# First expert unit by eight products, attention output with block pairs on the partitions, later weight loads

## The chip, the cores and the metric

The kernel runs on one core of one Trainium2 chip. The metric is the device time of one execution in microseconds (us). Before the change the median of three runs is 710.21 us (707.49 to 710.64). One execution more was recorded by the hardware profiler; all rows of a profile below come from that one.

## What is computed

Attention over 8 batches, 8 heads, 576 positions and 64 features a head, followed by a layer of 8 experts in which each token uses one expert.

```python
scores = q @ k.T / sqrt(64)           # heads 0-3: the last 32 positions
attn   = softmax(where(mask, scores, -1e9))   # heads 4-7: every 4th of the last 128
x      = (attn @ v) -> (B, S, 512)    # heads side by side

logits = x @ w_gate                   # 8 experts
local  = sigmoid(x @ w_local)
for s in order:                       # per batch
    e = argmax(logits[s]) if s == 0 or local[s] < 0.5 else e_of_the_token_before
    out[s] = softmax(logits[s])[e] * (relu(x[s] @ w1[e]) @ w2[e])
```

w1 of an expert is 512 x 1024, w2 is 1024 x 512, both float32 (2 MB each). A token's expert depends on its predecessor's where `local` is 0.5 or more, so that the routing is a scan along the sequence.

## The kernel before, in words

**Attention.** The program runs over 32 pairs of heads (`NPB`; four pairs a batch, two of plain heads and two of dilated heads, the latter sorted by position modulo 4 so that their windows are contiguous too). A pair has 9 query blocks of 64 positions (`NB`); a block sees 96 keys: 32 before it and its own 64. The loop at lines 1016 to 1044 runs 34 iterations n. In each:

- `scores(n)` (L284): for each block and head of the pair a product of keys and queries with the mask added, then the exponential on ScalarE. The blocks go in two groups (`UNITS`, 0 to 4 and 5 to 8).
- `values(n-1)` (L339): for each block and head the product of the probabilities (96 keys x 64 queries) with the values (96 x 65; the 65th column is ones and gives the sum). The two heads of the pair lie on partitions 0-63 and 64-127 of the PSUM tile `pv`. VectorE takes the reciprocals (L355) and multiplies (L356) into the tile `x`.
- `turn` (L360), in every second iteration from n = 3: transposes of `x` of two pairs (half a batch: 4 heads, 256 features), nine of 128 x 128, with ScalarE's copies into `xt`, the features of two batches. After four turns (two batches, a group g of four) the routing of the group is put into a queue (`route`, L976).
- `store` (L376): `x` of two pairs goes to the DRAM tensors `xd`, whose rows are tokens with 256 features (1024 bytes). With heads on the partitions each row is written in two pieces of 512 bytes.
- `load(n+3)` on SP's queue: keys and queries of a pair (592 KB) and values (292.5 KB). A block also needs the last 32 values of the block before it: GpSimd copies these "shared rows" within the tile (L247), as the last step of the load, so the copy of pair n+3 stands on GpSimd's queue in iteration n.

**Routing.** The queue `waiting` holds the steps of a group's routing (logits, L384, then the scan, the counting and the placing of tokens), each with an estimated cost. `gap(SHARE)` puts steps between the parts of an iteration as far as a credit allows; after the attention `work_gap()` puts one step, or a group that goes together, between two products of the experts. A second queue, `soon`, holds VectorE's sums, which `work_gap` takes when the queue of steps is empty or has an odd length.

**Experts.** Tokens are collected by expert into units. Units of kind "pair" are 256 tokens. They are computed with seven products in place of eight (`chain`, L820): the two operands are cut into quarters, sums of quarters are formed on VectorE (`sums_of_weights` for w1 and w2, `sums_right` in `features` for the tokens, called xc, `sums_left` for the hidden values, called hc; L766 to L775), and results are added up on VectorE (L891, L965). `hidden(u)` is relu(x w1), `output(u)` the product with w2; `features(u)` transposes the gathered rows of x (`xg`, by indirect DMAs on GpSimd, L797) into `xe`. Units 0 and 1 (`FIRST` = 2) take tokens of the first four batches only, so they can be formed while the attention still runs: after the second routing `early_tokens` puts their eight gathers into `rows`, of which each iteration of the attention issues one. The other units wait for the whole routing (`late_tokens`). A unit of kind "full" has 128 tokens and is computed directly, "half" has 64.

**Weights.** Three slots hold w1 (`raw1`) and w2 (`raw2`). The first w1 of slot 0 comes in four parts of 512 KB (`load_first`, n = 4, 6, 8, 10). At n = `NPB - 4` = 28 SP issues w2 of unit 0 and w1 of unit 1, 2 MB each; from n = 28 on, one sum of w1 of unit 0 is put into each iteration; at n = 30 come the features of unit 0, ahead of that iteration's end; w2 of unit 1 follows the attention.

**What sets the order.** TensorE, VectorE and GpSimd execute in the order of the program text; SP's queue issues DMAs in the order of the text as well. So every call above has a fixed place in the queue of each engine that it uses.

After the attention: `run_hidden(0)` with the sums of w2 of unit 0, features(1), `run_output(0)` with the sums of w1 of unit 1, `run_hidden(1)`, `output(1)`, in whose fourth product `feed` loads the weights of the next units and issues features(2); then the loop over the other units.

Of the kernel before, what the change touches and what calls it, by code (L numbers as in the profile page):

```python
# [38 lines left out]
UNITS = ((0, 5), (5, 9))  # L39
CB = 3  # L40
# [152 lines left out]
def whole(ctx, tc, exact, bad, qk, v, wgl, w1, w2, con, msk, qmk, out, cst, wg, ones):  # L193
# [35 lines left out]
    rec = once.tile([P, NPB, NB], F32, name="rec")  # L229
# [14 lines left out]
    def load_values(n):  # L244
        vt = vts[n % AHEAD]
        nc.sync.dma_start(out=vt[WIN:].rearrange("p u i e -> p (u i e)"), in_=v[n])
        nc.gpsimd.tensor_copy(vt[:WIN, :, 1:], vt[QB:, :, :NB - 1])  # L247
# [91 lines left out]
    def values(n):  # L339

        vt = loaded[n][2]
        if n % 2 == 0:
            xs[n // 2] = xp.tile([P, NB, 2, DH], F32, name="x")
        x = xs[n // 2]
        pr = prob.pop(n)
        for a, z in UNITS:
            pv = bank([P, z - a, VW], "pv")
            for i in range(a, z):
                c, p = next((c, p) for c, p in reversed(pr) if c <= i)
                for u in range(2):  # L350
                    nc.tensor.matmul(pv[u * QB:(u + 1) * QB, i - a], lhsT=p[:, u, (i - c) * QB:(i - c + 1) * QB],  # L351
                                     rhs=vt[:, u, i], start=True, stop=True, tile_position=(0, u * QB),
                                     skip_group_check=True)
            r = rec[:, n, a:z]
            nc.vector.reciprocal(r, pv[:, :, DH])  # L355
            nc.vector.tensor_tensor(x[:, a:z, n % 2], pv[:, :, :DH],  # L356
                                    r.unsqueeze(2).to_broadcast([P, z - a, DH]), op=Alu.mult)
        del loaded[n]

    def turn(m):  # L360

        x = xs[m]
        b, g = divmod(m, 2)
        if m % (2 * GB) == 0:
            routes[b // GB] = dict(xt=xtp.tile([P, 2, GS, CH], F32, name="xt"))
        xt = routes[b // GB]["xt"]
        w = NB // 3
        for c in range(3):
            tp = bank([P, w, 2, QB], "tp")
            for i in range(w):  # L370
                nc.tensor.transpose(tp[:, i].rearrange("p u q -> p (u q)"),
                                    x[:, c * w + i].rearrange("p g d -> p (g d)"), ident)
            s = b % GB * S + c * w * QB
            nc.scalar.copy(xt[:, g, s:s + w * QB].rearrange("p (i q) u -> p i u q", i=w), tp)

    def store(m):  # L376
# [3 lines left out]
        to = xd[g][b * S:(b + 1) * S].rearrange("(i q) (u f) -> u q i f", q=QB, u=2)  # L380
        for u in range(2):
            nc.sync.dma_start(out=to[u], in_=x[u * QB:(u + 1) * QB].rearrange("q i g d -> q i (g d)"))

    def logits(g):  # L384
# [4 lines left out]
        for kk in range(DK):  # L389
            for c in range(NC):  # L390
                if kk < CH:
                    rhs = xt[:, 0, c * NQ:(c + 1) * NQ, kk]
                else:
                    b, s = divmod(c * NQ, S)
                    rhs = xt[:, 1, b * S:(b + 1) * S, kk - CH].rearrange("p (c j) -> p j c", c=DIL)
# [301 lines left out]
    units = [dict(kind="pair", col=2 * i, slot=i, late=False) for i in range(FIRST)]  # L697
# [47 lines left out]
    def work_gap(sums=True):  # L745
        if waiting:
            gap()
            sums = sums and len(waiting) % 2
        for _ in range(len(soon) > 4 and 2 or len(soon) > 0 if sums else 0):
            soon.pop(0)()  # L750
# [35 lines left out]

    def gather(u):
        now(rows_of(u))

    def rows_of(u):  # L790
# [10 lines left out]
        return [lambda j=j, g=g, what=what: part(j, g, what) for j in range(2 if units[u]["kind"] == "pair" else 1)  # L801
                for g, what in enumerate(("tok", "pos"))]

    def features(u):
# [3 lines left out]
        for j in range(2 if kind == "pair" else 1):  # L808
# [37 lines left out]
    def hidden(u):  # L846
# [3 lines left out]
        if kind == "half":  # L850
# [7 lines left out]
            nc.scalar.activation(h[:, 0:2].rearrange("p m t -> p (m t)"), t, Act.Relu)  # L858
            return
# [53 lines left out]
    def output(u):  # L913
        i, kind = units[u]["slot"], units[u]["kind"]
        h, w = ht.pop(u), raw2[i]
        if kind == "half":
# [17 lines left out]
            return  # L934
        if kind == "full":
# [40 lines left out]
    def route(g, slow):  # L976
        steps = [(logits, 0, True), (fresh, 3.0, True), (carry, 1.0, True), (carry_over, 0.5, True), (carry_in, 0.5, True),
                 (choose, 1.5, True), (gate, 1.5, False), (place, 0.5, True), (lanes_of, 1.3, False)]
        if slow:
            waiting.insert(0, (lambda: logits(g), 0, True))  # L980
# [35 lines left out]
    for n in range(NPB + 2):  # L1016
        if n < NPB:
            (scores_exact if exact else scores)(n)
        gap(SHARE)
        if 1 <= n <= NPB:  # L1020
            values(n - 1)
        if n == NPB - 4:
            soon.extend(sums_of_weights(0, False))
        if soon:
            soon.pop(0)()
# [9 lines left out]
        if n in (4, 6, 8, 10):  # L1035
            load_first(0, n // 2 - 2)
        if n == NPB - 4:
            weights(0, True)
            weights(1, False)
        if rows:  # L1040
            rows.pop(0)()
        if n == NPB - 2:
            assert len(rows) <= 4
            now(features(0))
# [14 lines left out]
    def check():  # L1059

        flat = rec.rearrange("p n i -> p (n i)")
        fine = stage.tile([P, D], F32, name="y", bufs=3)[:, :NPB * NB]
# [8 lines left out]
        nc.vector.tensor_scalar(all_fine, lp, float(P * NPB * NB), None, Alu.is_lt)  # L1071
# [7 lines left out]
    def run_hidden(u, push):  # L1079
        soon.extend(push)  # L1080
        for fits in hidden(u):
            work_gap(fits)
        flush()
# [29 lines left out]
    run_hidden(0, sums_of_weights(0, True))  # L1113
    first, then = units[0]["sums"][:2], units[0]["sums"][2:]
    now(first)
    then += features(1)
    now(then)
    run_output(0, sums_of_weights(1, False))
    run_hidden(1, sums_of_weights(1, True))
    now(units[1]["sums"])  # L1120
    for k, fits in enumerate(output(1)):
        work_gap(fits)
# [4 lines left out]
    weights(after[1], True)  # L1127
    third = next(u for u in range(NU) if units[u]["slot"] == 2)
    for u in range(FIRST, NU):
# [8 lines left out]
        else:  # L1138
            now(push)
# [26 lines left out]
def _chunks(w):  # L1166

    return w.reshape(2, 2, CH, DH, -1).transpose(0, 2, 1, 3, 4).reshape(DK, P, -1)
# [33 lines left out]
```

## Time and profile before

| what | before |
|---|---|
| median of three runs | 710.21 us (707.49 to 710.64) |
| the profiled execution | 706.11 us, span of its instructions 703.9 us |
| mean granted clock of TensorE | 0.979 |
| busy: TensorE (PE) / weight loads (PEld) | 671.1 us (95%) / 579.1 us (82%) |
| busy: VectorE (DVE) / ScalarE (ACT) / GpSimd (POOL) | 386.2 (55%) / 194.8 (28%) / 183.5 us (26%) |
| DMA | 126.59 MB, mean 180 GB/s |
| attention, with its last logits | up to 173.59 us |

How to read the rows. A line of a timeline gives the start, the length, the engine, the line of the kernel, the operation, the tiles as written<-read, the shapes and how many instructions were merged into it; in brackets stands how long the engine had been idle before it, and what ended that. A float32 product leaves two records (x36 for 18 products); a transpose leaves one. The lengths of TensorE's instructions overlap, so the cost of a run of them is the distance of its start to the start of what follows. A line of stretches gives the stretch, its length, the busy time of each engine with its number of instructions, the granted clock (1.00 is full speed), the share of the DMA engines and GB/s. In the page's slices each digit is a fortieth of the span, in tenths.

### The profile page before, as it was taken

The numbers are of one execution on the slowest core, as the hardware profiler recorded it, in microseconds if no ns is written. First come the engines' busy times: TensorE is split into PE (matmuls) and PEld (weight loads), VectorE is DVE, ScalarE is ACT, GpSimd is POOL, SyncE is SP. The second block draws the span as 40 slices with busy tenths as digits, with TensorE's granted clock in tenths as the row PEclk, the third lists the DMA queues.
The fourth block names the chain that finished last, engine by engine and source line by source line (L and its number), as shares of the span: only waits on it lengthen the run. The fifth ranks groups of instructions, "written<-read, shape, count | busy, mean of one in ns | idle before, by whom it ended". The sixth has DMA issues, their size and how long they took to land. (4 is left out here: it accounts for less than half of the span.)

```text
span 703.9 us, 14739 instructions
## 1 busy us (share of the span) xinstructions
PE 671.1 (95%) x6182; PEld 579.1 (82%) x6182; DVE 386.2 (55%) x768; ACT 194.8 (28%) x353; POOL 183.5 (26%) x162
## 2 busy tenths in 40 slices
PE   8999999979997979999999999999999999999994
PEld 6977788756986978999689999599998699996883
DVE  3547478566697558544274572547461828442632
ACT  3544344322311232312122322222222132121220
POOL 3222212230012430402371331513133323032101
PEclk9999999966999999999999999999999999999998
DMA  8999878893102677567262614754004556342201
GB/s 330 321 342 284 250 235 256 257 349 83 73 16 104 226 265 274 184 250 266 84 267 73 229 38 151 245 203 168 31 23 128 217 181 251 135 170 57 122 23 35
DMA packets 38475, 126.59 MB, mean 180 GB/s; under 512 B 4253, under 2 KB 22813, under 8 KB 34432
## 3 DMA queue, kind: packets, MB, share of 16 engines
q1 hardware_dynamic: 31552, 106.15, 43.7%
q0 software_dynamic: 6848, 19.41, 8.0%
q8 instruction: 51, 0.84, 0.5%
q14 instruction: 24, 0.20, 0.1%
HBM read 142.32 MB, written 19.40 MB: 230 GB/s over the span
## 5 line engine op out<-in xcount | busy, mean ns | idle before, releaser
L909 POOL DMA_INDIRECT out_dram<-y,tok x36 | 53.9, 1497 | 323.0 <-DVE y L965 177.5
L881 PE MATMUL hp<-xc,sum 128*128 128x128 f32 x768 | 91.5, 275 | 1.2 <-DVE sum L766 1.2
L950 PE MATMUL yp<-sum,hc 128*128 128x256 f32 x384 | 88.5, 380 | 3.8 <-DVE hc L766 3.4
L881 PEld LDWEIGHTS hp<-xc,sum 128*128 128x128 f32 x768 | 88.5, 192 | 1.4 <-DVE sum L766 1.4
L891 DVE TENSOR_TENSOR h<-hp,h 128x512 f32<-128x512 f32 x48 | 32.9, 689 | 100.1 <-PE hp L881 97.8
L950 PEld LDWEIGHTS yp<-sum,hc 128*128 128x128 f32 x384 | 72.6, 190 | 14.5 <-DVE hc L766 3.4
L881 PE MATMUL hp<-xe,raw 128*128 128x128 f32 x512 | 62.9, 276 | 2.5 <-ACT xe L813 2.5
L881 PEld LDWEIGHTS hp<-xe,raw 128*128 128x128 f32 x512 | 60.2, 192 | 5.2 <-ACT xe L813 2.8
L247 POOL COPY vt<-vt 32x1040 f32<-32x1040 f32 x32 | 34.3, 1073 | 108.0 <-DMA vt<-in_v_dram 86.1
L950 PE MATMUL yp<-raw,h 128*128 128x256 f32 x256 | 60.7, 380 | 0.0
L301 PEld LDWEIGHTS two<-kq 64*96 64x96 f32 x1152 | 53.5, 167 | 7.8 <-issue 7.1
L301 PE MATMUL two<-kq 64*96 64x64 f32 x1152 | 58.0, 254 | 0.0
L965 DVE SCALAR_TENSOR_TENSOR y<-yp,gate,y 128x256 f32<-128x256 f32 x48 | 23.1, 482 | 58.6 <-issue 33.3
L950 PEld LDWEIGHTS yp<-raw,h 128*128 128x128 f32 x256 | 47.3, 190 | 6.1 <-issue 0.4
L797 POOL DMA_INDIRECT xg<-xd,tok x40 | 45.5, 1137 | 23.4 <-PE yp L950 10.6
L306 DVE SCALAR_TENSOR_TENSOR pr<-two,mk 96x512 f32<-96x512 f32 x32 | 21.9, 685 | 52.7 <-ACT pr L308 39.6
L892 ACT ACTIVATE h<-h 128x512 f32<-128x512 f32 x48 | 30.2, 630 | 71.3 <-DVE h L891 64.0
L885 ACT COPY h<-hp 128x512 f32<-128x512 f32 x48 | 28.1, 586 | 74.5 <-PE hp L881 73.3
L797 POOL DMA_INDIRECT xg<-xd,pos x40 | 42.9, 1072 | 12.2 <-issue 11.0
L351 PE MATMUL pv<-vt,pr 96*64 96x65 f32 x1152 | 43.1, 231 | 0.0
L958 ACT ACTIVATE y<-yp,gate 128x256 f32<-128x256 f32 x48 | 22.8, 474 | 66.2 <-PE yp L950 65.1
L351 PEld LDWEIGHTS pv<-vt,pr 96*64 96x64 f32 x1152 | 38.5, 144 | 2.5 <-issue 0.7
(208 smaller groups left out, 1005.1 us busy)
## 6 DMA issues: line engine op xcount, KB each, us to landing
raw<-in_w_dram SPq DMA_DIRECT2D x48, 2048.0 KB
kq<-in_qk_dram SPq DMA_DIRECT2D x32, 592.0 KB
vt<-in_v_dram SPq DMA_DIRECT2D x32, 292.5 KB
xd<-x SPq DMA_DIRECT2D x32, 288.0 KB
raw<-in_w_dram SPq DMA_DIRECT2D x4, 512.0 KB
xg<-xd,tok POOLq DMA_INDIRECT x40
xg<-xd,pos POOLq DMA_INDIRECT x40
out_dram<-y,tok POOLq DMA_INDIRECT x36
```

The lines of the kernel that those rows point to most:

```text
L247: nc.gpsimd.tensor_copy(vt[:WIN, :, 1:], vt[QB:, :, :NB - 1])
L301: nc.tensor.matmul(sc[:KW, u, (i - a) * QB:(i - a + 1) * QB], lhsT=kt[h, i * QB:i * QB + KW], rhs=qt[h, i * QB:(i + 1) * QB], start=bool(a ...
L351: nc.tensor.matmul(pv[u * QB:(u + 1) * QB, i - a], lhsT=p[:, u, (i - c) * QB:(i - c + 1) * QB], rhs=vt[:, u, i], start=True, stop=True, ti ...
L797: nc.gpsimd.indirect_dma_start(out=x[:rows, g], out_offset=None, in_=xd[g] if units[u]["late"] else xd[g][:EARLY * GS], in_offset=bass.Ind ...
L881: nc.tensor.matmul(to[:, m], lhsT=a[:, m, kk], rhs=b[:, kk], start=first and m == 0 and kk == 0, stop=(kk == DK // 2 - 1), skip_group_chec ...
L885: nc.scalar.copy(at((0, 1, 3)[k]), of)
L891: nc.vector.tensor_tensor(at(k), of, at(k), op=Alu.add)
L892: nc.scalar.activation(at(k), at(k), Act.Relu)
L909: nc.gpsimd.indirect_dma_start(out=out, out_offset=bass.IndirectOffsetOnAxis(ap=of_unit(u, "tok", j), axis=0), in_=y, in_offset=None, boun ...
L950: nc.tensor.matmul(to, lhsT=a[:, m], rhs=b[:, m], start=first and m == 0, stop=(m == FK // 2 - 1), skip_group_check=True)
L958: nc.scalar.activation(at(k), of, Act.Copy, scale=of_unit(u, "gate", k // 2))
L965: nc.vector.scalar_tensor_tensor(at(k), of, of_unit(u, "gate", k // 2), at(k), Alu.mult, Alu.add)
```

## The change

- **x and values.** `x` becomes [128, 5 slots, 2 pairs, 2 heads, 64]: on partitions 0-63 lies block 2k, on 64-127 block 2k+1. The fifth slot has only block 8; its second half computes block 8 again. The groups are `HALVES`, slots 0-1 and 2-4.
- **turn** makes eight transposes of 128 x 128 and two of 64 x 128, and three copies without a permutation; `xt` has the tokens innermost. **store** issues one DMA for 512 tokens and one for 64, in rows of 1024 bytes. Logits read `xt` with a step of one element in place of two (for the dilated heads: four classes 144 elements apart in place of 288). The weights' features are ordered to match, on the host.
- **Shared rows**: `share(n)` is called after `scores(n)`, no longer in the load of pair n.
- **Unit 0** is of the new kind "plain": 256 tokens with all products, 32 of 256 columns for hidden (two accumulations a PSUM bank) and 16 of 512 for output, without sums; ScalarE scales the output.
- **Later**: the four parts of the first w1 at n = 11, 14, 17, 20; w1 of unit 1, then w2 of unit 0, at n = 33; features(0) at n = 33, before the turn; no sums in the attention.
- **Order of the first units**: features(1) after hidden(0), its sums in output(0); the first two hc sums of unit 1 before the rest of `soon`; of output(1) the last two products go behind hidden(2), features(3) and gather(4), and the load of w2 of unit 3 behind them.
- `work_gap` always takes a step of the routing, and a sum where that step's cost is below 1.2; the last group's logits are issued at once.

```diff
@@ values
-            xs[n // 2] = xp.tile([P, NB, 2, DH], F32, name="x")
+            xs[n // 2] = xp.tile([P, SLOTS, 2, 2, DH], F32, name="x")
...
-        for a, z in UNITS:
-            pv = bank([P, z - a, VW], "pv")
-            for i in range(a, z):
-                c, p = next((c, p) for c, p in reversed(pr) if c <= i)
+        for a, z in HALVES:
+            pv = bank([P, z - a, 2, VW], "pv")
+            for k in range(a, z):
                 for u in range(2):
...
+                    for h in range(2):
+                        i = min(2 * k + h, NB - 1)
+                        c, p = next((c, p) for c, p in reversed(pr) if c <= i)
+                        nc.tensor.matmul(pv[h * QB:(h + 1) * QB, k - a, u], lhsT=p[:, u, (i - c) * QB:(i - c + 1) * QB],
+                                         rhs=vt[:, u, i], start=True, stop=True, tile_position=(0, h * QB),
+                                         skip_group_check=True)
@@ turn
+        s = b % GB * S
+        full = S // P * P
+        for c in range(CH):
+            tp = bank([P, S // P, P], "tp")
+            for k in range(S // P):
+                nc.tensor.transpose(tp[:, k], x[:, k, c].rearrange("p u d -> p (u d)"), ident)
+            nc.scalar.copy(xt[:, g, c, s:s + full], tp.rearrange("p k t -> p (k t)"))
+        tp = bank([P, CH, S - full], "tp")
+        for c in range(CH):
+            nc.tensor.transpose(tp[:, c], x[:S - full, S // P, c].rearrange("p u d -> p (u d)"),
+                                ident[:S - full, :S - full])
+        nc.scalar.copy(xt[:, g, :, s + full:s + S], tp)
@@ store
+        nc.sync.dma_start(out=to[:full].rearrange("(k p) f -> p k f", p=P),
+                          in_=x[:, :S // P].rearrange("p k g u d -> p k (g u d)"))
+        nc.sync.dma_start(out=to[full:], in_=x[:S - full, S // P].rearrange("p g u d -> p (g u d)"))
@@ units
-    units = [dict(kind="pair", col=2 * i, slot=i, late=False) for i in range(FIRST)]
+    units = [dict(kind="pair" if i else "plain", col=2 * i, slot=i, late=False) for i in range(FIRST)]
@@ work_gap
-        if waiting:
-            gap()
-            sums = sums and len(waiting) % 2
-        for _ in range(len(soon) > 4 and 2 or len(soon) > 0 if sums else 0):
+        before = credit[0]
+        gap()
+        for _ in range(len(soon) > 4 and 2 or len(soon) > 0 if sums and before - credit[0] < 1.2 else 0):
@@ hidden
+        if kind == "plain":
+            for m in range(FK):
+                if m % 2 == 0:
+                    t = bank([P, 2, 2 * P], "hp")
+                for kk in range(DK):
+                    nc.tensor.matmul(t[:, m % 2], lhsT=w[:, m, kk], rhs=x[:, kk], start=(kk == 0), stop=(kk == DK - 1))
+                if m % 2:
+                    nc.scalar.activation(h[:, m - 1:m + 1], t, Act.Relu)
+                yield True
+            return
@@ output
+        if kind == "plain":
+            for j in range(2):
+                yp = bank([P, D], "yp")
+                for m in range(FK):
+                    nc.tensor.matmul(yp, lhsT=h[:, m, j * P:(j + 1) * P], rhs=w[:, m], start=(m == 0), stop=(m == FK - 1))
+                    if m % 2:
+                        yield True
+                y = stage.tile([P, D], F32, name="y", bufs=3)
+                nc.scalar.activation(y, yp, Act.Copy, scale=of_unit(u, "gate", j))
+                send(y, u, j)
+            return
@@ the loop of the attention
+        if n < NPB:
+            share(n)
         gap(SHARE)
         if 1 <= n <= NPB:
             values(n - 1)
-        if n == NPB - 4:
-            soon.extend(sums_of_weights(0, False))
-        if soon:
-            soon.pop(0)()
+        if n == NPB + 1:
+            assert len(rows) <= 4
+            now(features(0))
...
-        if n in (4, 6, 8, 10):
-            load_first(0, n // 2 - 2)
-        if n == NPB - 4:
+        if n in (11, 14, 17, 20):
+            load_first(0, (n - 11) // 3)
+        if n == NPB + 1:
+            weights(1, False)
             weights(0, True)
-            weights(1, False)
         if rows:
             rows.pop(0)()
-        if n == NPB - 2:
-            assert len(rows) <= 4
-            now(features(0))
@@ run_hidden
+        if not units[u]["late"] and units[u]["kind"] == "pair":
+            now(units[u]["sums"][:2])
         flush()
@@ the first units
-    run_hidden(0, sums_of_weights(0, True))
-    first, then = units[0]["sums"][:2], units[0]["sums"][2:]
-    now(first)
-    then += features(1)
-    now(then)
-    run_output(0, sums_of_weights(1, False))
+    run_hidden(0, [])
+    push = features(1)
+    run_output(0, sums_of_weights(1, False) + push)
     run_hidden(1, sums_of_weights(1, True))
-    now(units[1]["sums"])
-    for k, fits in enumerate(output(1)):
-        work_gap(fits)
+    soon.extend(units[1]["sums"][2:])
+    rest = output(1)
+    for k in range(FEED + 2):
+        work_gap(next(rest))
         if k == FEED:
             feed()
             soon.extend(sums_of_weights(FIRST, False))
     flush()
-    weights(after[1], True)
...
-            now(push)
+            soon.extend(push)
+            for fits in rest:
+                work_gap(fits)
+            flush()
+            weights(after[1], True)
```

## The prediction

> **What bounds the kernel now.** I read the page's slices, then the groups by shape, then the stretches and TensorE's timeline wherever a slice shows it idle.
>
> ```profile
> PE   8999999979997979999999999999999999999994
> PEclk9999999966999999999999999999999999999998
> ```
>
> TensorE is the bound (671.1 of 703.9 us, the page's first part); no other engine is above 55%. So added TensorE work costs its full time, and a gain can only come from TensorE's idle time and from its clock, which dips in slices 9 and 10. The stretches, with the busy times of PE, PEld, DVE, ACT and POOL and the granted clock, show where the rest is lost:
>
> ```profile
> 10.00:138.06 128.06, 125.28 (x2361) 104.56 (x2357) 79.02 (x247) 56.12 (x100) 32.32 (x31) 1.00 0.90 285
> 138.06:173.59 35.53, 28.60 (x338) 21.72 (x334) 24.33 (x68) 9.45 (x18) 8.80 (x9) 0.66 0.65 212
> 205.20:239.66 34.46, 29.54 (x210) 27.34 (x208) 24.96 (x75) 7.18 (x13) 14.91 (x11) 1.00 0.35 114
> 239.66:271.66 32.00, 27.55 (x241) 26.93 (x240) 20.56 (x26) 10.09 (x18) 7.74 (x8) 1.00 0.76 297
> ```
>
> A clean iteration of the attention, from TensorE's timeline (start, length):
>
> ```profile
> 15.73 0.47 PE L296 MATMUL two<-mk 96*96 96x320 bf16 x2
> 17.80 1.27 PE L351 MATMUL pv<-vt,pr 96*64 96x65 f32 x36
> 19.01 1.20 PE L371 MATMUL tp<-cst,x 128*128 128x128 f32 x9
> 20.05 0.44 PE L296 MATMUL two<-mk 96*96 96x320 bf16 x2
> ```
>
> By the starts: scores 2.07 us, values 1.21, a turn 1.04. The same work at the end of the attention, and the transposes of unit 0's features (L812) among it, with the idle time ahead of each and what ended it:
>
> ```profile
> 142.69 1.14 PE L371 MATMUL tp<-cst,x 128*128 128x128 f32 x6 [0.59 <-ACT xt L374]
> 154.92 1.19 PE L812 MATMUL tp<-cst,xg 128*128 128x128 f32 x4 [4.21 <-DMA xg<-xd,tok]
> 156.57 3.15 PE L301 MATMUL two<-kq 64*96 64x64 f32 x36
> 159.65 2.22 PE L351 MATMUL pv<-vt,pr 96*64 96x65 f32 x36
> 168.31 1.30 PE L371 MATMUL tp<-cst,x 128*128 128x128 f32 x9 [1.75 <-DVE x L356]
> ```
>
> GpSimd shows why the gathered rows came late: the copy of the shared rows stands ahead of the gathers.
>
> ```profile
> 147.38 1.04 POOL L247 COPY vt<-vt 32x1040 f32<-32x1040 f32 x1 [6.58 <-PE op L460]
> 148.69 0.96 POOL L797 DMA_INDIRECT xg<-xd,tok  x1 [0.27 <-POOL vt L247]
> ```
>
> The PE that is named fits no operand of the copy; its other wait is for the DMA of the values, issued at 138.21, just before 4 MB of weights at 138.98. And behind the attention:
>
> ```profile
> 221.11 2.05 PE L881 MATMUL hp<-xc,raw 128*128 128x128 f32 x16 [1.70 <-DVE h L891]
> 228.32 3.72 PE L950 MATMUL yp<-sum,hc 128*128 128x256 f32 x16 [2.98 <-DVE hc L766]
> 255.75 2.05 PE L881 MATMUL hp<-xe,raw 128*128 128x128 f32 x16 [2.55 <-ACT xe L813]
> 258.96 3.28 PE L881 MATMUL hp<-xc,sum 128*128 128x128 f32 x27 [1.16 <-DVE sum L766]
> ```
>
> **Values, turn and store: dearer.** With nine blocks in five slots, block 8 is computed twice: 20 products a pair for 18, two records each. 1.21/36 = 0.0336 us a record, four more are 0.13 us, times 32 pairs = 4.3 us, all on TensorE's path. A turn has 8 full and 2 half transposes for 9: at 0.116 each (1.04/9), and 0.11 for a half (the 64x64 form of L812, 1.8 us for 16), 1.15 us; 16 turns add 1.7. VectorE's multiplies become 256 and 384 elements for 320 and 256: by the two rows (492 and 424 ns) 68 ns a pair, 2.2 us; most of it lies under TensorE (VectorE 79 of 128 us), I charge 0.5. ScalarE copies 512, 512 and 128 elements for three of 384 (1.51 us): about 1.45. Logits read the same stride pattern with half the pitch: first half of the 32 records 1.14 us, second (four classes apart) 2.1. Between nothing and 1 us less in each of four; the elements stay far apart, so nothing. Stores keep two issues a batch and halve their packets; nothing waits for them in the attention, so zero, and no cover is lost. Sum +6.5 (5 to 8).
>
> **The end of the attention: the largest gain.** Clean work from 138.06 to 173.59: 3 scores 6.2, 4 values 4.8, 3 turns 3.1, features 1.0, logits 3.2 (at 42.84), routing's small products 1.3: 19.6 of 35.5 us. The excess is 15.9: 6.9 of it idle (0.59 + 0.34 + 4.21 + 1.75), the rest the half clock. What made it is moved. The four sums of unit 0's weights (1.22 us each on VectorE, which held up the turn at 142.69) are gone. The copy of shared rows is issued one pair ahead, its data three pairs old, so POOL has nothing to wait for and the gathers behind it go one an iteration. The values that need a copy follow one iteration later: 3.3 us of cover for 1.05 us of copy and 1 us of gather, so the new place costs nothing; without that cover each pair would lose up to 1 us. features(0) comes three iterations later and has its rows. It now stands between the last values and the last turn, so its 0.95 us of transposes cover half of the 1.75 us wait for x.
>
> Moved past SP's queue: four 512 KB loads from 24-51 us to some 53-99 us, where the DMA share is 0.66 to 0.98; their room comes from the halved store packets, and loads run three pairs ahead (zero; 2 us if not). The two 2 MB loads now stand behind the last store, w1 of unit 1 ahead of w2 of unit 0, and on SP only w2 of unit 1 is queued behind them, which is needed some 40 us later. Then 0.6 + 2.1 + 2.1 MB must land before output(0). At 300 GB/s (between 401 and 253, the rates at 140 to 160) that is 16 us; TensorE has features (1.0), turn (1.2), logits (3.2), a routing product (2.7) and the hidden products (13.8, below) to do first, with waits some 23 us. Slack 7; a load later than that would stop TensorE, and all behind it, us for us.
>
> What can be left is the clock. The rule that speaks against this change is in the Trainium skill, "TensorE: Matmul & The Clock Gate", Part 4: a PE transpose doesn't count as PE being busy; by Part 1 of it a window of about 3.4 us without enough work halves the clock. The trace agrees in the time: 0.50 from 145.4 to 165.9, six windows of 3.41. The change puts 18 transposes and their copies, 2.9 us, ahead of the logits. By the rule a window closes and the logits and first hidden product lose 1.7 us; by the row at 55.22 (transposes and idle from 53.2 to 55.7, clock 1.00) nothing. I take 0.8. The rule also says one busy window reopens the clock; here scores and values ran from 155.9 to 165.7 at 0.50, so a closed gate in the attention is worse than the page makes it. Waits for copies: 1.0. Net -14.1 (-16 to -8).
>
> **Unit 0 plain.** Hidden: 64 records at 0.216 (1.73 for 8, L950) = 13.8 for 7 x 1.785 = 12.5; output: 32 at 0.441 (L938, 7.06 for 16) = 14.1 for 12.1. +3.3 on the path. VectorE loses 8 sums (9.8), xc 1.7, hc 2.7, adds 3.5.
>
> **Waits of units 0 to 3.** TensorE idles 10.4 us from 173.59 to 271.66. hc and y of unit 0 (0.42, 0.33) vanish. 1.70 and 2.98 are VectorE's backlog: routing's late count, tokens and unit 1's sums ahead of hc. Now it has 11 us less to do from 173 on (four sums of w2, hc, adds), hidden and output give 16 gaps for 14, so the tokens come before hidden(1) ends, and hc's first two sums are pushed ahead of the rest. 2.55 and 1.16 (xe, the first sum of unit 3) get a cover: the last two products of output(1), 3.46 us. Its weights load goes behind w1 of unit 4 on SP, 13 us ahead of need. If the backlog stayed, 4.7 would remain; features(1) and its sums now lie in output(0), under 14 us of products. Left: 0.26 + 0.24 + 0.74 and 1.3 for new waits = 2.5. Net -7.9 (-3 to -9).
>
> **Sum.** +6.5 - 14.1 + 3.3 - 7.9 = -12.2. The profiled execution took 706.1 us (span 703.9), so 693.9; the median of the runs is 710.2, 4.1 above it. On that median: **698.0**. About 0.5% (3.6 us) is what a measurement of this kernel can tell from no change.
>
> **Rivals.**
> - The backlog only moves (20%): VectorE stays full through hidden(1), or output(0) waits for w2 of unit 0. For it: VectorE 24.96 of 34.46. The 4.7 us come back: 702.7.
> - The clock closes at a turn of the last iterations (12%): scores and values then cost 3.09 + 2.22 for 1.68 + 1.27 us, with the turn some 3 us an iteration; three iterations, 9 us: 707. For it: it happened at 145.4, after a longer string of transposes. Against: idle behind that string is removed.
> - Slower (5%): the same gate closes in a routing iteration early on, and the small products don't reopen it. At 3 us each, it decides from (12.2 + 3.6)/3, five to six iterations; from the second routing (iteration 20) to 31 it is 12, 36 us: 734. Against: 1.00 from 10 to 145 us, and the turn grows by 0.1 us only.
> - Better (7%): the doubled block is partly hidden (-3), the logits gain (-3) and no gate closes (-1): 691.
>
> The likeliest has 56%, 693 to 702. With the backlog, most of the better case and half of the gate's in it, the range is 689.5 to 706, which leaves out some 15 in 100. Faster 0.87 (likeliest, backlog, better, a third of the gate's), same 0.08 (the rest of the gate's), slower 0.05.
>
> **What would show it.** Right: L351 near 40 records in 1.34 us; no gap at features(0); clock 1.00 to the last values; no wait for hc in output(1); hidden(3) starting without xe's wait. Wrong: POOL's copy still idle for a DMA at the end, a granted clock of 0.5 for more than one window, a wait for raw at output(0), or TensorE waiting on VectorE's sums in hidden(1).

## The result, and the profile after

The changed kernel takes 700.65 us in the median of 20 runs (694.28 to 709.75), the kernel before 708.64 us in 20 runs beside them: ratio 0.987, 95% interval 0.9844 to 0.9895. The prediction said 698.0 on 710.2, a ratio of 0.983. The profiled execution took 699.44 us, span 697.7, mean granted clock 0.989. (Runs more than 1.5% above the fastest of their kernel are left out of all ratios, but not out of the medians and spreads.)

The two lines of slices of the page after:

```profile
PE   8999998998999899999999999999999999999995
PEclk9999999899999999999999999999999999999998
```

TensorE's three slices at 7 are gone; the clock reads 9 (90% or more) in slices 9 and 10 and dips in slice 8, where it was full before. The stretches, cut where the program starts the scores of iteration 29, hidden(0) (at 173.49), hidden(1), hidden(2) and the features of unit 4 (the prediction's last stretch ends behind these features, which start at 270.79 before the change):

```profile
10.00:147.53 137.53, 133.91 (x2492) 112.64 (x2491) 81.49 (x247) 55.80 (x101) 29.35 (x29) 0.98 0.82 266
147.53:173.49 25.96, 22.80 (x356) 17.78 (x354) 18.88 (x60) 8.79 (x18) 10.22 (x10) 0.93 0.65 210
206.50:234.66 28.16, 26.31 (x194) 24.27 (x193) 19.25 (x69) 7.52 (x13) 10.98 (x11) 1.00 0.35 126
234.66:265.67 31.01, 29.83 (x249) 29.07 (x248) 22.39 (x30) 9.23 (x16) 5.81 (x6) 1.00 0.56 219
```

Set against before: the attention reaches iteration 29 some 9.5 us later (147.53 for 138.06), its end is 9.6 us shorter (25.96 for 35.53), so that hidden(0) starts at the same time (173.49 for 173.59). From there to the features of unit 4 it takes 92.2 us for 97.2, and the rest 432.0 for 433.1. In these two executions all of the gain lies behind the attention. In a clean iteration:

```profile
18.77 1.39 PE L358 MATMUL pv<-vt,pr 96*64 96x65 f32 x40
20.08 1.09 PE L379 MATMUL tp<-cst,x 128*128 128x128 f32 x8
21.11 0.34 PE L383 MATMUL tp<-cst,x 64*128 64x64 f32 x2
```

Values take 1.31 us for 1.21, a turn 1.29 for 1.04 (21.37, the next start, less 20.08). And four places on TensorE that the prediction did not have:

```profile
117.23 0.30 PE L383 MATMUL tp<-cst,x 64*128 64x64 f32 x2 [1.50 <-DVE rec L362]
122.44 4.79 PE L569 MATMUL ap<-lane,what 96*112 96x128 f32 x24
163.88 2.41 PE L358 MATMUL pv<-vt,pr 96*64 96x65 f32 x38 [0.86 <-POOL vt L252]
169.07 1.15 PE L379 MATMUL tp<-cst,x 128*128 128x128 f32 x8 [1.23 <-ACT xe L828]
```

The small transposes wait 1.50 us for VectorE's reciprocals (the tile `rec`) in a routing iteration; from some 119.5 to 126.5 the clock is 0.50, and the routing's product takes 4.79 us for 2.87. Values(31) wait for GpSimd's copy of the shared rows, and one more window closes (164 to 167.4).

**Why the reciprocals are late.** VectorE's mask of the routing (L554) at two places, and GpSimd at the second:

```profile
73.15 0.84 DVE L554 TENSOR_TENSOR is_it<-cst,segs 96x672 f32<-96x672 f32 x1
...
115.11 1.42 DVE L554 TENSOR_TENSOR is_it<-cst,segs 96x672 f32<-96x672 f32 x1
```

```profile
114.78 1.04 POOL L252 COPY vt<-vt 32x1040 f32<-32x1040 f32 x1 [3.10 <-PE pv L358]
```

The copy starts 0.33 us before the mask and the mask lasts 0.58 us longer, of the 0.71 that were left of the copy; no copy runs beside the mask of 73.15. The Trainium skill, "SBUF — State Buffer" (SBUF: two separate sides), says that VectorE, reading two operands from SBUF, and GpSimd share a pair of ports that one of them holds for its whole instruction; the rows agree. The reciprocals stand behind the mask. In x2 below, which differs from the changed kernel only in the place of the copies, the mask takes 0.84 us at both places and the transposes of that turn (at 113.00) wait for no reciprocal.

**Why the copy is late at the end.** GpSimd and SP in the last iterations:

```profile
158.06 0.97 POOL L812 DMA_INDIRECT xg<-xd,tok  x1 [0.27 <-POOL vt L252]
162.79 1.04 POOL L252 COPY vt<-vt 32x1040 f32<-32x1040 f32 x1 [3.75 <-PE kp L518]
```

```profile
159.60 0.81 SPq L741 DMA_DIRECT2D raw<-in_w_dram  x1
```

In the compiled program each copy that stands behind a gather waits for the landing of that gather, besides the DMA of its own values. The last packet of the gather of 158.06 lands at 162.23 and the copy starts at 162.79; the four copies before it start 0.47 to 0.48 us behind the last packet of the gather ahead of each. In x2 the profile names the wait:

```profile
145.28 1.06 POOL L249 COPY vt<-vt 32x1040 f32<-32x1040 f32 x1 [2.33 <-DMA xg<-xd,pos]
```

One pair ahead this leaves no cover. The gather of 158.06 met the 2 MB of w1 of unit 1 at 159.60 and landed 4.17 us after its start, the two gathers before it 2.43 us. The text has that load behind the last store (169.19); SP's queue did not keep the order of the text, and the load went out ahead. The prediction, and the text ahead of it, took SP's order for that of the text, and the copy of 147.38 in the kernel before for one that waited for its values: it stood behind a gather too.

### The profile page after: what moved, and what is told of

It is laid out like the page before. It is cut to its first block, busy times and chain, and to the rows that moved or that the text cites. A ratio compares the mean times of both kernels' runs of the same rounds, so it can differ in the third digit from the quotient of the medians.

```text
span 697.7 us, 14846 instructions
## 1 busy us (share of the span) xinstructions
PE 676.3 (97%) x6254; PEld 577.7 (83%) x6254; DVE 373.9 (54%) x746; ACT 190.6 (27%) x348; POOL 183.5 (26%) x162
## 5 line engine op out<-in xcount | busy, mean ns | idle before, releaser
L906 PE MATMUL hp<-xc,sum 128*128 128x128 f32 x720 | 85.7, 275 | 1.2 <-DVE sum L778 0.7
L906 PEld LDWEIGHTS hp<-xc,sum 128*128 128x128 f32 x720 | 82.9, 192 | 1.6 <-issue 0.9
L986 PE MATMUL yp<-sum,hc 128*128 128x256 f32 x360 | 82.8, 380 | 0.4 <-DVE sum L784 0.4
L986 PEld LDWEIGHTS yp<-sum,hc 128*128 128x128 f32 x360 | 68.2, 190 | 10.2 <-DVE sum L784 0.8
L906 PE MATMUL hp<-xe,raw 128*128 128x128 f32 x480 | 58.9, 276 | 0.0
L906 PEld LDWEIGHTS hp<-xe,raw 128*128 128x128 f32 x480 | 56.5, 192 | 1.5 <-issue 1.2
L986 PE MATMUL yp<-raw,h 128*128 128x256 f32 x240 | 56.8, 380 | 0.0
L986 PEld LDWEIGHTS yp<-raw,h 128*128 128x128 f32 x240 | 44.4, 190 | 5.8 <-issue 0.4
L358 PE MATMUL pv<-vt,pr 96*64 96x65 f32 x1280 | 46.8, 230 | 0.9 <-POOL vt L252 0.9
L358 PEld LDWEIGHTS pv<-vt,pr 96*64 96x64 f32 x1280 | 42.1, 143 | 3.4 <-POOL vt L252 1.0
```

The lines of the kernel that those rows point to most:

```text
L358: nc.tensor.matmul(pv[h * QB:(h + 1) * QB, k - a, u], lhsT=p[:, u, (i - c) * QB:(i - c + 1) * QB], rhs=vt[:, u, i], start=True, stop=True, ...
L906: nc.tensor.matmul(to[:, m], lhsT=a[:, m, kk], rhs=b[:, kk], start=first and m == 0 and kk == 0, stop=(kk == DK // 2 - 1), skip_group_chec ...
L986: nc.tensor.matmul(to, lhsT=a[:, m], rhs=b[:, m], start=first and m == 0, stop=(m == FK // 2 - 1), skip_group_check=True)
```

## Experiments

All ratios are to the kernel before, run beside each. The clock is called closed or shut where the granted clock is 0.50, and open where it is 1.00. "Half clock" is the time at half clock per execution, 2 x (1 - mean clock) x span, as the median of the runs that the ratio uses; it is 28 to 30 us for the kernel before and 15.4 for the changed one. Of it, 3 to 8 us lie at the very end of the program in every profile (682.5 to 687.1 in x10).

| kernel | median us | ratio (95%) | half clock | profile: scores(29) / hidden(0) starts / from there to the end |
|---|---|---|---|---|
| before | 708.6 | 1 | 28 to 30 | 138.1 / 173.6 / 530.3 |
| changed | 700.65 | 0.987 (0.9844 to 0.9895) | 15.4 | 147.5 / 173.5 / 524.2 |
| x1 old layout | 697.7 | 0.9847 (0.9817 to 0.9878) | 15.3 | 138.7 / 171.2 / 524.3 |
| x2 copies 3 pairs ahead | 700.8 | 0.990 (0.9873 to 0.9926) | 20.9 | 141.2 / 174.0 / 524.3 |
| x3 early weights | 703.9 | 0.9942 (0.9917 to 0.9966) | 22.4 | 142.4 / 174.6 / 524.1 |
| x4 unit 0 by seven | 710.2 | 1.0019 (0.9996 to 1.0042) | 34.0 | 142.7 / 181.9 / 528.2 |
| x5 late copies on ScalarE | 716.0 | 1.0084 (1.0052 to 1.0116) | 43.6 | - / 182.6 / 529.3 |
| x6 = x1 + x5 | 701.5 | 0.9867 (0.9836 to 0.9897) | 19.6 | - / 170.0 / 530.6 |
| x7 gathers last | 708.9 | 0.9997 (0.9976 to 1.0019) | 29.0 | - / 187.1 / 530.8 (an execution of 719.9 us) |
| x8 long turns | 724.1 | 1.0184 (1.0146 to 1.0223) | 25.3 | - / 198.2 / 525.9 |
| x9 routing behind turn | 703.7 | 0.9967 (0.994 to 0.9993) | 25.2 | - / 176.1 / 522.8 |
| x10 paced gathers | 689.6 | 0.9735 (0.9688 to 0.9781) | 4.1 | 141.7 / 164.1 / 523.0 |
| x11 all three | 688.4 | 0.9723 (0.9678 to 0.9767) | 8.2 | - / 161.7 / 524.9 |
| x12 old layout, paced | 687.3 | 0.9738 (0.9693 to 0.9784) | 5.5 | 145.7 / 168.3 / 524.5 (an execution of 694.6 us) |

**x1, the layout undone.** The five functions that touch `x` as before, the rest as changed:

```diff
-        for a, z in HALVES:
-            pv = bank([P, z - a, 2, VW], "pv")
+        for a, z in UNITS:
+            pv = bank([P, z - a, VW], "pv")
```

> The changed kernel with x, values, turn, store and logits as they were before: 18 products a pair in place of 20, nine whole transposes a turn in place of eight and two halves, x written in pieces of 512 bytes. All other parts of the change stay. Theory (the new layout is a cost on TensorE's path, 3.6 us for the products and 4.0 us for the turns, and its halved packets relieve nothing that TensorE waits for): 5 to 9 us faster than the changed kernel, some 693 us; values back at 1.21 us, a turn at 1.04, and no longer wait at output(0) of unit 0. Rival (the larger packets are what lets the later weights land in time): the two 2 MB loads behind the attention land later, hidden(0) or output(0) waits for raw, and the time is within 2 us of the changed kernel or above it.

Measured: 697.7 us, by the ratios 1.6 us below the changed kernel, though the intervals overlap. TensorE is at scores(29) 2.5 to 4.0 us ahead of the four kernels of the new layout whose clock was open up to there (x2, x3, x4, x10), so the layout is a cost, but no more than that. By kind of work: the first 29 pairs of values take 35.8 us (38.2 in x2), the first 13 turns 18.8 us (18.4 in x2, 18.3 in x10). The old turn is the shorter one only where nothing else goes on; beside routing it waits for banks, and takes 1.4 to 2.1 us. Then it lost what it had won: w1 of unit 1 was issued at 152.57, right behind a gather, and

```profile
152.09 0.97 POOL L802 DMA_INDIRECT xg<-xd,tok  x1 [0.27 <-POOL vt L250]
159.46 1.04 POOL L250 COPY vt<-vt 32x1040 f32<-32x1040 f32 x1 [6.39 <-issue]
```

```profile
160.56 2.00 PE L354 MATMUL pv<-vt,pr 96*64 96x65 f32 x32 [5.15 <-POOL vt L250]
```

values(31) waited 5.15 us and the clock was shut from 158.9 to 169.1. The later loads landed as before: nothing waited for raw. In the attention the theory is right in sign and too large in size. The rival's wait for raw did not come, but its time, within 2 us of the changed kernel, did.

**x2, the copies back in the load** (three pairs ahead):

```diff
-        if n < NPB:
-            share(n)
@@ load
+        nc.gpsimd.tensor_copy(vt[:WIN, :, 1:], vt[QB:, :, :NB - 1])
```

> The changed kernel with the copy of the shared rows back in the load, three pairs ahead; all else as changed. Theory A (the copy's place made the 4.21 us of idle time before the change, by keeping the gathers behind it): the copies idle on GpSimd for the values' DMA again, each gather goes later, features(0) waits for its rows in iteration 33 or the gathers run into it; 2 to 6 us slower than the changed kernel. Theory B (each copy waits for the gather ahead of it as well, and with three pairs of cover that wait is hidden, where one pair ahead shows it as 0.86 us before values(31)): the wait of values(31) vanishes, features(0) at n = 33 has its rows anyway, and the time is within 1.5 us of the changed kernel, either side.

Measured: 700.8 us, ratio 0.990: theory B by the median and by the wait of values(31), which is gone; by the ratios it is 2 us above the changed kernel, with intervals that overlap. The copy's place, which the change makes much of, is worth nothing that these runs show by itself. But the gain of the cover was eaten by something new. GpSimd had no copy between the last six gathers, which ran from 146.62 to 153.83 without a pause, and TensorE, in the middle of values(30):

```profile
150.09 0.38 PE L355 MATMUL pv<-vt,pr 96*64 96x65 f32 x5 [0.37 <-issue]
150.83 0.34 PE L355 MATMUL pv<-vt,pr 96*64 96x65 f32 x4 [0.36 <-issue]
151.56 0.22 PE L355 MATMUL pv<-vt,pr 96*64 96x65 f32 x1 [0.40 <-issue]
152.27 0.53 PE L355 MATMUL pv<-vt,pr 96*64 96x65 f32 x4 [0.49 <-issue]
153.71 0.46 PE L355 MATMUL pv<-vt,pr 96*64 96x65 f32 x3 [0.91 <-issue]
```

It starts and stops, waiting for nothing that the profile shows; VectorE and ScalarE stood too (busy 1.19 and 0.63 of the 5.9 us from 149.7). The clock closed at 152.2 for 17.1 us.

**x3, early weights.**

```diff
-        if n in (11, 14, 17, 20):
-            load_first(0, (n - 11) // 3)
-        if n == NPB + 1:
+        if n in (4, 6, 8, 10):
+            load_first(0, n // 2 - 2)
+        if n == NPB - 4:
             weights(0, True)
```

> The changed kernel with the weights loaded when they were before: the four 512 KB parts at n = 4, 6, 8, 10, w2 of unit 0 and w1 of unit 1 at n = 28. Theory A (the two loads of 2 MB at n = 28 made the gathered rows and values late, so moving them is a part of the gain): the DMA of values(31) and the gathers land 5 us or more after their issue again, values or features wait, 2 to 5 us slower. Theory B (the unit's features at n = 33 and the missing sums carry the gain; the loads' place is worth nothing): within 1.5 us of the changed kernel.

Measured: ratio 0.9942, 5 us above the changed kernel by the ratios: theory A. The 4 MB went out at 143.31, right behind the gather of 143.15, and the next copies, behind gathers, came late:

```profile
152.18 1.83 PE L358 MATMUL pv<-vt,pr 96*64 96x65 f32 x38 [1.92 <-POOL vt L252]
```

**x4, unit 0 by seven products** (`kind="pair"` for all units, its sums from n = 28 on):

```diff
+        if n == NPB - 4:
+            soon.extend(sums_of_weights(0, False))
+        if soon:
+            soon.pop(0)()
@@ the first units
-    run_hidden(0, [])
+    run_hidden(0, sums_of_weights(0, True))
+    soon.extend(units[0]["sums"][2:])
```

> The changed kernel with unit 0 by seven products again: sums of its w1 in iterations 28 to 31 of the attention (with the weights only arriving by the new times), sums of its w2 in hidden(0), the rest of hc in output(0); all else as changed. Theory A (VectorE is what the end of the attention and units 0 to 3 waited for, and eight products buy 10 to 15 us of VectorE for 3.3 us of TensorE): TensorE's own work falls by 3.3 us, but waits for sums, hc and x come back, some 5 to 9 us of them, and the time is 2 to 6 us above the changed kernel. Theory B (the order of the first units and of the queues is what removed the waits): 2 to 3.5 us faster than the changed kernel.

Measured: 710.2 us, all of the gain gone, more than theory A asked. Hidden(0) starts 8.4 us later than in the changed kernel (values waited 4.35 us for a copy, the clock was shut from 154 to 181.5), and from there on it takes 528.2 us for 524.2, though unit 0 has 3.3 us less work: hidden(1) waited for VectorE.

```profile
217.61 2.50 PE L906 MATMUL hp<-xc,sum 128*128 128x128 f32 x16 [3.87 <-DVE xc L784]
```

**x5, the last four copies on ScalarE**, and **x6**, the same on the old layout:

```diff
+        if n < NPB - 4:
+            nc.gpsimd.tensor_copy(vt[:WIN, :, 1:], vt[QB:, :, :NB - 1])
+        else:
+            nc.scalar.copy(vt[:WIN, :, 1:], vt[QB:, :, :NB - 1])
```

> The changed kernel with the copies of the shared rows of the last four pairs (28 to 31) on ScalarE in place of GpSimd; all else as changed. Theory A (a copy on GpSimd behind a gather waits for that gather's landing, and the values behind it, with TensorE's clock, pay for that): no wait of values on the shared rows at the end, fewer closed stretches there; 1.5 to 4 us faster than the changed kernel, 697 to 699. Theory B (something at the end stops TensorE anyway, and ScalarE, which the exponentials go through, gets 1 us more an iteration): within 1.5 us of the changed kernel, or slower.

> The changed kernel with the old layout of x (18 products, nine whole transposes, pieces of 512 bytes) and the last four copies of shared rows on ScalarE. Theory A (the two causes add: the layout costs about 4 us of TensorE in the attention, the copies behind gathers some 2 to 5 us with the clock): 690 to 694 us, and no idle time of TensorE over 2 us before hidden(0). Theory B (TensorE's clock closes once at the end whatever comes first, so the second saving is lost): 696 to 698 us, as with the old layout alone.

Both theories fell: 716.0 us, and 701.5, no better than x1. No values waited for shared rows, but seven gathers now ran in a row (146.18 to 154.69 in x5, 135.39 to 143.90 in x6), and TensorE had the same broken run of small starts, from 149.7 to 156.3 and from 138.9 to 145.5. In x5 the small transposes also waited 1.23 us for `rec` at 74.67, long before anything of the edit, and the clock was shut for 17 us:

```profile
PEclk9999689978999999999999999999999999999998
```

**x7, all gathers behind the last copy:**

```diff
-        if rows:
-            rows.pop(0)()
+        if n >= NPB - 1:
+            for _ in range(min(len(rows), 4)):
+                rows.pop(0)()
```

> The changed kernel with the eight early gathers issued from iteration 31 on, all behind the last copy of shared rows on GpSimd. Theory A (copy waits for gather): no wait of values on the shared rows; features(0) still has its rows; 1.5 to 4 us faster than the changed kernel. Theory B (gathers in a row hold up every engine, as in the run with the copies three pairs ahead, where TensorE had seven gaps of 0.4 to 1.0 us between 149.7 and 155.1 while six gathers stood in a row on GpSimd): the same gaps come at the end, 3 to 4 us of them, the clock closes, and the time is that of the changed kernel or 1 to 3 us above.

Measured: 708.9 us. Theory B, and more: eight gathers from 156.63 to 166.46, gaps of 0.2 to 1.1 us from 159.8 to 168.1 with about 5 us of idle time, and the clock shut from 163.7 to 184.2. In this profile it had been shut for 17 us from 78.4 on as well, behind a wait of 2.04 us for `rec`. Where theory B had the time of the changed kernel or 3 us more, it is 9 us more by the ratios.

In x5 to x8 hidden(2) waited as well, 2.1 to 4.6 us, at its first products with a sum of unit 2 (0.4 to 1.6 in the other profiles of changed kernels). I did not settle why; it is in their last column and hides nothing of the above.

**x8, the rule on transposes:**

```diff
+        if m in (2, 5, 10):
+            tp = bank([P, S // P, P], "more")
+            for i in range(64):
+                nc.tensor.transpose(tp[:, i % 4], x[:, i % 4, i % CH].rearrange("p u d -> p (u d)"), ident)
```

> The changed kernel with 64 more transposes of 128 x 128 in front of the turns of iterations 7, 13 and 23; their results are not used, and the kernel's output is the same. 64 at 0.116 us are 7.4 us, 22.3 for the three. Theory A (transposes count as work for the clock): 1.00 at all three places, 722 to 724 us. Theory B (the page's rule, transposes don't count and one busy window reopens): each place closes the gate; the second half of the transposes is slower (1.7 us) and one window of 3.4 us behind it goes at half clock (1.7 us): 733. Theory C (they don't count, and the small products of the attention don't reopen it, as from 155.9 to 165.7 us before the change): 0.50 for 15 to 20 us behind each place, 6 to 8 us more each, 745 to 755.

Measured: 724.1 us, theory A. TensorE's stretches of these transposes alone, the clock in the third column from the end:

```profile
36.16:43.37 7.21, 7.21 (x70) 7.21 (x67) 0.86 (x3) 0.23 (x1) 2.09 (x2) 1.00 0.85 273
71.53:78.74 7.21, 7.21 (x70) 7.21 (x67) 1.95 (x8) 0.23 (x1) 2.09 (x2) 1.00 0.86 270
```

7.2 us of float32 transposes, longer than two windows, leave the clock at 1.00, also after them. The rule of the Trainium skill, "TensorE: Matmul & The Clock Gate", Part 4, that a PE transpose doesn't count as PE being busy, does not hold for these. The clock closed at 167.2 and at 177.4, where values had waited 1.93 and 2.93 us for a copy.

**x9, the routing steps behind the turn:**

```diff
+        turns = n >= 3 and n % 2 == 1
+        if not turns:
+            gap(SHARE)
         if 1 <= n <= NPB:
             values(n - 1)
```

> The changed kernel with the routing steps of the iterations that have a turn put behind the turn (both shares of the credit there), so that VectorE's reciprocals and multiplies for the turn don't stand behind a routing step. Theory A (the small transposes of the turn wait for VectorE's work on values where a routing step stands ahead of it and is stretched by GpSimd's copy, 0.2 to 2 us, and such a wait of 1.2 us and more closes the clock for 10 to 17 us): waits of the small transposes on rec under 0.4 us, no stretch at 0.50 before iteration 29; 3 to 5 us faster than the changed kernel, 695.5 to 698, with less spread. Theory B (the wait moves to the next iteration's exponentials and closes the clock there): within 1.5 us of the changed kernel.

Measured: ratio 0.9967, 7 us above the changed kernel by the ratios. The waits on `rec` were 0.53 us at most and the clock was open up to 153, as asked; but two copies behind gathers (151.92 and 165.65) held up values by 1.37 and 2.31 us and the clock closed there. So with the first wait gone another one closed it. Theory A fell as far as the time goes.

**x10, paced gathers** (x2, and one element copied on GpSimd ahead of each gather, which waits for the values of that iteration):

```diff
         if rows:
+            if n <= NPB:
+                nc.gpsimd.tensor_copy(pace, rec[:1, n - 1, 0, :1])
             rows.pop(0)()
```

> The changed kernel with the shared rows copied in the load, three pairs ahead (as in the earlier run of that), and ahead of each early gather a copy of one element on GpSimd that waits for the values of the iteration: so the same gathers, one an iteration, instead of six in a row. Theory A (gathers in a row are what stops all engines for some 0.4 to 1 us at a time): no gaps of TensorE with nothing released in iterations 28 to 32, no wait of values on the shared rows, and at most one or two closed windows before hidden(0); 3 to 6 us faster than the run with six in a row, 695 to 698. Theory B (each gather stops the engines for its share wherever it stands): about 0.5 us of gaps behind each gather, the sum the same, 699 to 702.

Measured: 689.6 us, ratio 0.9735, better than both theories. The same gathers and copies as in x2:

```profile
147.24 0.97 POOL L809 DMA_INDIRECT xg<-xd,tok  x1 [0.15 <-POOL pace L1075]
148.55 0.97 POOL L809 DMA_INDIRECT xg<-xd,pos  x1 [0.16 <-issue]
151.14 0.97 POOL L809 DMA_INDIRECT xg<-xd,tok  x1 [0.48 <-issue]
155.91 0.97 POOL L809 DMA_INDIRECT xg<-xd,pos  x1 [0.48 <-issue]
```

```profile
141.67:164.14 22.47, 21.26 (x357) 16.15 (x353) 18.39 (x61) 9.08 (x18) 10.00 (x15) 1.00 0.71 229
```

No gaps, no wait on shared rows, the clock at 1.00 from scores(29) to hidden(0), 22.5 us for 32.8 in x2.

**x11 and x12, versions to beat both kernels:** x10 with the old layout and the routing behind the turn, and x10 with the old layout alone (the edits of x1, x9 and x10 together, and of x1 and x10).

> The old layout of x, the copies three pairs ahead with paced gathers, and the routing steps of a turn's iteration behind the turn; units, weights and the order of the first units as changed. Theory A (the layout's 4 us and the closed clock add): clock 1.00 up to hidden(0) but for at most one window, 688 to 692 us, faster than both kernels. Theory B (one closing at the end comes whatever is done, or the old layout's stores delay loads once the rest is shorter): 694 to 698.

> The run with paced gathers (copies three pairs ahead, one gather an iteration), with the old layout of x as well; routing steps where the changed kernel has them. It measures the layout where the clock stays open. Theory A (the new layout costs TensorE 3.6 us in the products of the values and 4 us in the turns, and nothing comes back for it): 6 to 8 us below the run with paced gathers, relative to the kernel before, hidden(0) starting at 157 to 158 us. Theory B (a part of it is hidden by waits, or the doubled number of packets costs something): 2 to 4 us below, hidden(0) at 160 to 162. Theory C (the new layout is worth its cost where the clock stays open, since the larger packets let loads land): not below it.

Measured: 688.4 and 687.3 us, ratios 0.9723 and 0.9738. Both beat the changed kernel by 1.3 to 1.5%; between x10, x11 and x12 the intervals (0.9% wide) decide nothing. x11 had waits of 1.41 and 2.16 us for `rec`, which left the clock open. x12's profile is of its slowest execution, whose clock was shut for 17 us from 74 on; from scores(29) to hidden(0) it took 22.5 us, as x10. So at the end of the attention the layout costs nothing that shows. The ratios of x10 and x12 are theory C's (not below it), but their width leaves room for theory B. The profiles lean to B: with the clock open all the way, x11 starts hidden(0) at 161.7, 2.4 us ahead of x10, but it has the edit of x9 as well. Some 3 us over the whole attention is the best value I have; which theory holds for the time stays open.

## Why the prediction was right, and which steps were not

- **Unit 0 plain and the waits of units 0 to 3: right.** +3.3 and -7.9 were to give -4.6 from hidden(0) to the features of unit 4; measured -5.0. TensorE's waits there fell from 10.4 to some 3.0 us (2.5 forecast), with none for hc, for xe at hidden(3), or for raw at output(0). x4 shows both sides: 3.3 us less of products, 4.0 more of time. In the profiled executions the gain of 6.2 us is this part and 1.1 us behind it, which the sum did not have.
- **The layout: right for the values, over-sized elsewhere.** Values: 3.1 us (38.2 less 35.1 us before, for 29 pairs), so 3.4 for 32 pairs; forecast 4.3. The turns: nothing; forecast 1.7. The clean turn does cost 0.25 us more, but most turns aren't clean: 13 of them took 18.4 us before and 18.3 to 18.4 in x10 and x2. Logits gained nothing (3.09 us), as taken. The sum of +6.5 was some 3.
- **The end of the attention, -14.1: the step that failed.** It brought -9.6. Ahead of it the attention lost 9.5 us, where the layout's 6.5 were forecast and some 3 are the layout's (scores(29) is at 141.7 in x10, whose clock stays open, and at 138.1 before); the rest are the waits and the closed clock, which was to be open there. So up to hidden(0) the sum had -7.6 and the profiled executions show -0.1, though the time at half clock up to there fell from 23.9 to 10.2 us. Two sentences were wrong. "POOL has nothing to wait for": each copy waits for the gather in front of it, and one pair ahead its cover of 3.3 us ends where the gather meets a load. And "what can be left is the clock, 0.8": a wait of 1.2 to 1.9 us closed it at five places (the changed kernel, x3, x5, x8, x9), for 3.4 to 17 us, since the attention's small products reopened it late. x10 shows that the step was sound in what was to be had: with the gathers paced and covered, hidden(0) starts at 164.1, where the sum had 166.
- **The rivals.** "The clock closes at a turn" (12%) and "in a routing iteration" (5%) both came true in part: at 119 in the profiled run, behind a wait on `rec`, once and for some 7 us, in place of the twelve iterations that would have made it slower. I had put 9 us and 36 us on them; over the 16 runs of the changed kernel that the ratio uses, the time at half clock is 8 to 25 us, and each of these costs about 0.4 (the spans follow 691.4 + 0.386 x half clock, r = 0.83). "The backlog moves" did not happen.
- **The rule on transposes** didn't matter and doesn't hold here (x8). The clock closed behind idle time, and transposes seem to help to open it. Counted over all 14 profiles from 10 to 660 us, the clock changes only at steps of 3.41 us. All 22 closings follow a step with 0.97 us or more of idle time on TensorE, but 23 such steps, with up to 1.97 us, did not close it, 18 of them among the experts' products: so no limit comes out. All 22 reopenings follow a step with next to no idle time (0.08 us at most) that held transposes or products on 128 partitions (in nine of them, transposes alone), or once the routing's products on 96; 15 unbroken steps of scores and values alone left it closed. So that one busy window reopens it (Part 1 of that page) is contradicted again: in x5 TensorE was busy at 0.50 from 76.5 to 93.6.

On the ratios the forecast was some 3 us too low: the clock and the waits took more than the layout gave back. That the time lies well inside the range does not speak for the largest term: the part behind hidden(0) was right, and the range was wide enough for the other.

## What to carry to other kernels

A row of gathers needs a pace, and what waits behind a gather needs a cover: pace alone (the changed kernel) and cover alone (x2) both took some 700 us, the two together (x10) 690. Where TensorE works in small products, price a wait not by its length but by what it may do to the clock, and look for it in every profile afresh, since small shifts decide whether two engines meet.

## What the runs showed that I had not expected

- Gathers back to back on GpSimd (one each 1.25 us) brought all engines to a stuttering stop about 3 us into the row, in x2, x5, x6 and x7; the starts on TensorE lie 0.72 us or twice that apart. In x10 the eight gathers start 1.3 to 7.6 us apart, with never more than two in a row at 1.3, and there was none. The kernel before had six in a row too (148.69 to 155.93), but there TensorE stood for 4.21 us waiting for gathered rows, so that a stop would not show. Twelve gathers in a row (212.6 to 228.3 us in x10), under products of 128 x 128 and 128 x 256, did not stop TensorE so. What is held up is not in the profile; that it is the supply of instructions is a guess (the Trainium skill, "DMA: Bandwidth & Descriptors", Queues, rings and completion order, has the runtime's refill on one of the rows that each DMA engine serves in turn; no run here shows it: in x2 a single packet of the two instruction queues starts between 147.20 and 159.72, at 154.03).
- A GpSimd copy of 1.04 us stretched VectorE's mask from 0.84 to 1.42 us, and VectorE's step before it (L544, at 110.73 in the changed kernel) from 0.94 to 1.75.
- The clock at 0.50 stayed so through 17 us of unbroken attention work.
